# Attention units of all token groups in one pipeline: scores and values in one TensorE section

## The chip, the cores and the metric

The kernel runs on one core of one Trainium2 chip. The metric is the device time of one execution in microseconds. The kernel before takes 826.89 us, the median of three runs (826.69 to 827.46).

## What is computed

The reference is masked attention followed by a token mixer and a channel mixer, for 8 batches of 576 tokens, 8 heads of 64. Heads 0 to 3 see the last 32 positions ("local"), heads 4 to 7 every 32nd earlier position ("strided"):

```python
scores = (1.0 / np.sqrt(D)) * np.matmul(q, k.transpose(0, 1, 3, 2))
mask_local = (rel >= 0) & (rel < 32)
mask_strided = (rel >= 0) & (pos[None, :] % 32 == pos[:, None] % 32)
attn = softmax(where(mask, scores, -1e9))
x = (attn @ v).transpose(0, 2, 1, 3).reshape(B, S, H * D)
h = np.maximum(x.transpose(0, 2, 1) @ w_tok1, 0.0) @ w_tok2
u = x + h.transpose(0, 2, 1)
out = u + np.maximum(u @ w_ch1, 0.0) @ w_ch2
```

## The kernel before

The channel mixer is most of the work. The 4608 tokens are cut into 9 groups of 512. For each group, mlp() (line 668) runs 12 up-projections (up_proj, L680) and 12 down-projections (down_proj, L699), of 12 matmuls of 128x512 each, since every fp32 product is made of three products of split halves. An up-projection accumulates in one of two PSUM banks of the pool ps_h; its result is read by ScalarE (gh, L685) and then by VectorE (gl, L686), and used by the down-projection two steps later. Four further banks hold the down-projection's sums, and the last two are the pool ps_t.

Between these matmuls mlp() has 48 slots for each group, four for each step fc: slot 4fc in the middle of up_proj(fc+2), 4fc+1 behind it and ahead of the reads gh and gl, 4fc+2 in the middle of down_proj(fc), and 4fc+3 behind it. Everything else for the next batch is inserted there by at(slot, function), and each engine runs its instructions in just this order, since the schedule is manual: attention units, the token mixer (tok1 at slots 31 to 41, tok2 around it), the loads of x, and in group 0 the conversion of the weights (convert at even slots, fetch at odd ones; ScalarE and VectorE rebuild and split each 128x512 piece, and a DMA on SyncE's queue brings the next).

An attention unit is a Python generator (local_unit L194, strided_unit L254) over two or three blocks of 128 rows and two heads. Its steps are: load q and k; scores, 24 or 48 small matmuls (L81) into two ps_t banks; on VectorE the masked scores with their minimum (L167) and on ScalarE the exponentials (L170), for each block and head; reciprocal of the sums and load of v; transposes on TensorE (L84) with a copy on ScalarE (L191); values, again 24 or 48 small matmuls (L81) into two ps_t banks; a product with the reciprocals on VectorE (L237, L291) into the tile ax; a store to DRAM. A later load_x reads the stored rows as x of the next batch. The framework puts two engines' accesses to one PSUM bank one behind the other.

In groups 0 and 1 there are eight units each, four strided and four local, one every three slots from slot 4. Unit k's scores stand at slot 4+3k, together with the transposes of unit k-1, which go into the free columns of the same two banks; its values stand five slots after its scores, in a section of their own. Groups 2 to 6 have three, three, three, three and two local units, one every five slots from slot 0, with the values eight slots after the scores. A stretch of TensorE work of this kind between matmuls of the mixer is called a section below. Batches 3 to 7 have their strided heads on GpSimd and VectorE (L345, L346, L393, L395), which don't use TensorE. The loads of x are issued from SyncE's queue at slots 28 and 31 (24 and 27 from group 2), behind the stores that they need. The output tiles of a group (result, L716) are taken from GpSimd's product tiles and from the local units' tile lv.

Of the kernel before, what the change touches and what calls it, by code (L numbers as in the profile page):

```python
# [26 lines left out]
P = 128  # L27
# [58 lines left out]

class Bank:
# [6 lines left out]
def attn_mixer_kernel(ctx, tc, qT, kT, vw, qs, ks, vs, qsT, ksT, vsP, mask, words, outT):  # L94
# [62 lines left out]
    def new_scores(work):  # L157
        small = [work.tile([P, 16], F32, name=name)[:, :2 * UC].rearrange("p (c j) -> p c j", j=2) for name in ("am", "az")]
        return work.tile([P, UC, 2, 64], F32, name="as"), *small
# [34 lines left out]
    def local_unit(pool, work, p, hp, c0, n, into=None, got=None):  # L194
# [28 lines left out]
        for t in range(4 * n):  # L223
            c, a = divmod(t, 4)
            for j in range(2):
                av[j].by.matmul(
                    av[j].of[32 * a:32 * a + 32, 64 * c:64 * c + 64],
                    pT[64 * j:64 * j + 64, 32 * t:32 * t + 32], v_t[64 * j:64 * j + 64, t], start=True, stop=True)
        x_t = new_out(work)
# [24 lines left out]
    def strided_unit(pool, work, b, hp, half, got=None):  # L254
# [28 lines left out]
        for t in range(UT):  # L283
            c, a = divmod(t, 2)
            for j in range(2):
                av[j].by.matmul(
                    av[j].of[64 * a:64 * a + 64, 64 * c:64 * c + 64],
                    pT[64 * j:64 * j + 64, P * c + 64 * a:P * c + 64 * a + 64], v_t[64 * j:64 * j + 64, t], start=True, stop=True)
        x_t = new_out(work)
# [246 lines left out]
    with tc.tile_pool(name="first", bufs=2) as first, \  # L536
# [68 lines left out]
        for k in range(n + 3):  # L605
            if k >= 3:
                units[k - 3].send(banks[k - 3])
            if 0 <= k - 2 < n:
# [52 lines left out]
    ps_h = Banks(tc, ctx.enter_context(tc.tile_pool(name="ps_h", bufs=2, space=PSUM, reuse_waits="tile")))  # L661
# [6 lines left out]
    def mlp(grp, us, inserts):  # L668
# [3 lines left out]
        def up_proj(fc, mid=lambda: None):  # L672
            fs = slice(P * fc, P * fc + P)
            ph = ps_h.tile("h")
# [31 lines left out]
        def out_tile(cc):  # L706
            if cc < NCC - 1:
                o_t = product(pools["sp"], (SPROD, D))
            else:
                o_t = late.tile([P, 4 * UC, D], F32, name="lv")[:, :GT // D]  # L710
            return o_t.rearrange("p a b -> p (a b)")
# [54 lines left out]
    def do_load(b, part):  # L766
        if part == 0:
            state["x"] = xp.tile([P, NSC, DM], F32, name="x", bufs=1)
            if b < NPE:
                load_x(state["x"], b, 1)  # L770
            load_x(state["x"], b, 0, 0, 2)
        else:
            load_x(state["x"], b, 0, 2)
            if b >= NPE:
                load_x(state["x"], b, 1)
# [39 lines left out]
    def group_units(b):  # L815
# [6 lines left out]
        return st[:1] + [u for k in range(4) for us_ in (st[1:], loc) for u in us_[k:k + 1]]  # L822

    made = {}
    all_units = [group_units(g + 1) for g in range(B - 1)] + [[], []]
    all_live = [[None] * len(u) for u in all_units]

    def load(g, k):
        all_live[g][k] = all_units[g][k]()
        next(all_live[g][k])  # L830

    for g in range(NG):
# [6 lines left out]
        def pair():  # L839
            return [ps_t.bank() for _ in range(2)]  # L840

        b = g + 1
        if b < B:
            units, live = all_units[g], all_live[g]
            first_, tick, half_tick, ahead = (4, 3, 2, 3) if g < 2 else (0, 5, 3, 4)
            def qk(k, live=live):
                banks = pair()
                u = live[k] if k < len(live) else None
                if u:
                    u.send(banks)  # L850
# [171 lines left out]
```

## Time and profile before

| | us |
|---|---|
| median of three runs | 826.89 |
| the profiled execution | 826.54 |
| its span, first to last instruction | 824.8 |
| TensorE busy | 799.4 (97%) |
| VectorE busy | 477.4 (58%) |
| ScalarE busy | 260.8 (32%) |
| GpSimd busy | 252.3 (31%) |
| chain that ended last, TensorE's share | 87% |

Matmuls overlap in the record: one of 128x512 is shown at 0.39 us, but the next starts some 0.227 us after it. What a section costs is therefore read from starts: from the last matmul of the mixer ahead of it to the first or second one behind it, less what these matmuls would take in a row.

### The profile page before, as it was taken

To read this page: it belongs to the slowest core of one execution; us is meant where nothing else is said; L and a number is where in the kernel's file an instruction comes from. 1 tells how busy PE (TensorE), PEld (TensorE's weight loads), DVE (VectorE), ACT (ScalarE), POOL (GpSimd) and SP (SyncE) were. 2 spreads that over 40 slices of the span, in tenths; PEclk is the share of its full clock that TensorE was granted. 3 is DMA by queue.
4 is the path that set the end of the run, shared out by engine and by line. 5 is a ranking of instruction groups with operands and counts; after the bars stand their busy time and mean duration, and the time that the engine had idled before them with its cause. 6 is when DMAs were issued, how large, how long until landed. Compare 5 with 4: busy or idle time off the path is not lost.

```text
span 824.8 us, 16436 instructions
## 1 busy us (share of the span) xinstructions
PE 799.4 (97%) x6360; PEld 649.3 (79%) x6360; DVE 477.4 (58%) x1694; ACT 260.8 (32%) x803; POOL 252.3 (31%) x258
## 2 busy tenths in 40 slices
PE   6899889999999999999999999999999999999998
PEld 5666668877788788878887888788878888888886
DVE  4887775445467668766786676766775324113122
ACT  6777773244322312231224121322131221101110
POOL 2300000042201792279426762578238100000000
PEclk9999999999999999999999999999999999999999
DMA  9546762234524231232314140515021301001001
GB/s 362 183 141 209 227 215 61 85 128 143 141 68 147 80 94 58 87 126 55 112 53 147 40 142 25 173 39 141 1 91 40 92 1 52 1 0 39 14 1 51
DMA packets 61905, 79.65 MB, mean 97 GB/s; under 512 B 16676, under 2 KB 47268, under 8 KB 61828
## 3 DMA queue, kind: packets, MB, share of 16 engines
q1 hardware_dynamic: 60404, 74.14, 28.6%
q0 software_dynamic: 1136, 4.06, 1.3%
q8 instruction: 50, 0.82, 0.4%
q10 hardware_dynamic: 288, 0.40, 0.1%
q14 instruction: 27, 0.22, 0.1%
HBM read 59.97 MB, written 18.48 MB: 95 GB/s over the span
## 4 chain that ended last, share of the span: by engine, by line
PE 87%; ACT 5%; DMA 3%; DVE 3%; issue 1%; SPq 0%; ACTq 0%; DVEq 0%
PE acc L699 34%; PE h L680 33%; PE t L81 19%; ACT as L170 2%; PE t L84 2%; DMA lv<-in_vw 1%; ACT w_raw L124 1%; DMA x<-ax 1%; DMA mask_sb<-in_mask 1%; DMA ek<-in_ksT 1%; ACT gh L685 1%; ACT w_a L122 0%; DMA w_raw<-in_words 0%; DVE w1l L153 0%; DVE gl L686 0%
## 5 line engine op out<-in xcount | busy, mean ns | idle before, releaser
L393 POOL TENSOR_TENSOR sprod<-sv,ss 128x512 f32<-128x512 f32 (+9 forms) x150 | 136.3, 949 | 137.0 <-DVE ss L369 101.1
L680 PE MATMUL h<-uh,w1h 128*128 128x512 f32 x432 | 171.9, 398 | 1.4 <-DVE ul L488 1.4
L699 PE MATMUL acc<-gh,w2h 128*128 128x512 f32 x432 | 172.5, 399 | 0.0
L699 PE MATMUL acc<-gh,w2l 128*128 128x512 f32 x432 | 168.7, 391 | 0.0
L680 PE MATMUL h<-uh,w1l 128*128 128x512 f32 x432 | 168.6, 390 | 0.0
L699 PE MATMUL acc<-gl,w2h 128*128 128x512 f32 x432 | 168.6, 390 | 0.0
L680 PE MATMUL h<-ul,w1h 128*128 128x512 f32 x432 | 168.5, 390 | 0.0
L686 DVE SCALAR_TENSOR_TENSOR gl<-h,gh 128x512 fp32r<-128x512 f32 x108 | 74.2, 687 | 132.4 <-ACT gh L685 131.8
L685 ACT ACTIVATE gh<-h 128x512 fp32r<-128x512 f32 x108 | 64.8, 600 | 257.4 <-PE h L680 257.3
L345 POOL TENSOR_TENSOR sprod<-sk,sq 128x512 f32<-128x512 f32 x80 | 101.9, 1305 | 135.6 <-DVE ss L346 96.3
L680 PEld LDWEIGHTS h<-uh,w1h 128*128 128x128 f32 x432 | 81.1, 188 | 19.5 <-DVE ul L488 2.2
L699 PEld LDWEIGHTS acc<-gh,w2l 128*128 128x128 f32 x432 | 81.1, 188 | 17.4
L680 PEld LDWEIGHTS h<-uh,w1l 128*128 128x128 f32 x432 | 81.1, 188 | 17.2
L699 PEld LDWEIGHTS acc<-gh,w2h 128*128 128x128 f32 x432 | 81.2, 188 | 16.6
L680 PEld LDWEIGHTS h<-ul,w1h 128*128 128x128 f32 x432 | 81.2, 188 | 15.8
L699 PEld LDWEIGHTS acc<-gl,w2h 128*128 128x128 f32 x432 | 81.3, 188 | 15.3
L395 DVE TENSOR_REDUCE so<-sprod 128x64 f32<-128x512 f32 (+9 forms) x150 | 73.5, 524 | 12.6 <-POOL sprod L393 11.8
L170 ACT ACTIVATE as<-as,am 128x64 f32<-128x64 f32 x216 | 72.3, 337 | 25.2 <-DVE am L167 23.0
L488 DVE TENSOR_TENSOR ul<-t,uh 128x512 fp32r<-128x512 f32 (+7 forms) x64 | 29.1, 457 | 71.7 <-ACT uh L487 71.7
L487 ACT CAST uh<-t 128x512 fp32r<-128x512 f32 (+7 forms) x64 | 25.6, 404 | 116.7 <-PE t L81 116.7
L346 DVE TENSOR_REDUCE ss<-sprod 128x8 f32<-128x512 f32 x80 | 52.2, 670 | 12.4 <-POOL sprod L345 12.2
L167 DVE CUSTOM_DVE_ANT_0 as<-t,mask_sb 128x64 f32<-128x64 f32 x216 | 34.5, 221 | 35.2 <-ACT as L191 21.9
(103 smaller groups left out, 928.7 us busy)
## 6 DMA issues: line engine op xcount, KB each, us to landing
w_raw<-in_words SPq DMA_DIRECT2D x21, 512.0 KB, 4.5
out_t<-sprod SPq DMA_DIRECT2D x27, 256.0 KB, 2.2
lv<-in_vw SPq DMA_DIRECT2D x18, 384.0 KB, 4.3
lk<-in_kT SPq DMA_DIRECT2D x18, 208.0 KB, 3.4
x<-xl SPq DMA_DIRECT2D x14, 256.0 KB, 4.4
lq<-in_qT SPq DMA_DIRECT2D x18, 192.0 KB, 3.1
xl<-ax SPq DMA_DIRECT2D x18, 192.0 KB
sq<-in_qs SPq DMA_DIRECT2D x5, 576.0 KB
```

The lines of the kernel that those rows point to most:

```text
L81: self.tc.stamp_issue_order_token(self.tc.nc.tensor.matmul(*args, **how).ins, self.pool.name)
L167: nc.vector.tensor_tensor_reduce(out=s_t[:, c, j, :], in0=sc[j].of[:, 64 * c:64 * c + 64], in1=mask_sb[:, m, :], scale=-SCALE, scalar=TOP, ...
L170: nc.scalar.activation(out=s_t[:, c, j, :], in_=s_t[:, c, j, :], func=AF.Exp, bias=m_t[:, c, j:j + 1], scale=-1.0, accum_out=z_t[:, c, j:j ...
L345: nc.gpsimd.tensor_tensor(out=pr, in0=k_t[:, n0:n0 + n], in1=q_t[:, i:i + 1].to_broadcast([P, n, D]), op=ALU.mult)
L346: return [lambda: nc.vector.tensor_reduce(out=s_t[:, i, n0:n0 + n], in_=pr, axis=AX.X, op=ALU.add)]
L393: nc.gpsimd.tensor_tensor(out=pr, in0=v_t[:, d0:d1, :n], in1=s_t[:, n - 1:n, :n].to_broadcast([P, d1 - d0, n]), op=ALU.mult)
L395: todo.append(lambda n=n, d0=d0, d1=d1, pr=pr: nc.vector.tensor_reduce(out=o_t[:, n - 1, d0:d1], in_=pr, axis=AX.X, op=ALU.add))
L488: nc.vector.tensor_tensor(out=ul, in0=pu, in1=uh.bitcast(F32), op=ALU.subtract)
L680: nc.tensor.matmul(ph, l[:, cc, fs], r, start=(cc == 0 and k == 0), stop=(cc == NCC - 1 and k == 2))
L685: nc.scalar.activation(out=gh, in_=ph, func=AF.Relu)
L686: nc.vector.scalar_tensor_tensor(out=gl, in0=ph, scalar=0.0, in1=gh.bitcast(F32), op0=ALU.max, op1=ALU.subtract)
L699: nc.tensor.matmul(acc[cc], l[:, fc, cs], r, start=(fc == 0 and k == 0), stop=(fc == NFC - 1 and k == 2))
```

## The change

All 30 units of all groups become one list with one list of 32 sections: slots 4, 7, ..., 31 of group 0, 4, 7, ..., 25 of group 1, then 4, 11 and 18 of groups 2 to 5, and 4 and 11 of group 6. Strided and local units of groups 0 and 1 now alternate strictly. Section n has, in TensorE's order, the values of unit n-2 in columns 0 to 191 of two ps_t banks, the scores of unit n in columns 192 to 383 of the same banks and, up to section 16, the transposes of unit n-1 in the bank of ps_h that the up-projections don't use at that moment. Behind that, VectorE takes the scores first and the values' product second. From unit 16 on the scores of unit k and the values of unit k-1 share a section, and the transposes stand alone in a ps_t bank, four slots after the scores (seven after those at slot 18).

The two banks of ps_h get names, h0 and h1. Turns.next() alternates between them; Turns.spare(turn) hands out the bank that is not in use: at slots 4fc and 4fc+1 (turn 0) the one whose up-projection has been read before, at 4fc+2 and 4fc+3 (turn 1) the same, with the turn flipped, so that the next up-projection goes into the bank of the up-projection just before it.

Loads of q and k move from three (or four) slots ahead of the scores to four (five); v is loaded two (three) slots after the scores, as before. The loads of x stand at slots 28, 30 and 33 in groups 0 and 1 (24, 27, 27 later), with the strided half second. A group's last values in group 0 stand at slot 31 and the strided ones at 28 (before: 30 and 24). The minima am have one buffer and the sums az three in these pools (before: two each). Output tiles are taken from the tiles xh and xlo of tok1.

```diff
--- before.py
+++ after.py
@@ -84,6 +84,19 @@
         self.tc.stamp_issue_order_token(self.tc.nc.tensor.transpose(*args).ins, self.pool.name)
 
 
+class Turns(Banks):
+
+    last = 0
+
+    def next(self):
+        self.last ^= 1
+        return self.tile(f"h{self.last}")
+
+    def spare(self, turn):
+        self.last ^= turn
+        return self.bank(f"h{self.last if turn else self.last ^ 1}")
+
+
 class Bank:
 
     def __init__(self, by, of):
@@ -155,7 +168,8 @@
 
 
     def new_scores(work):
-        small = [work.tile([P, 16], F32, name=name)[:, :2 * UC].rearrange("p (c j) -> p c j", j=2) for name in ("am", "az")]
+        bufs = {"am": 1, "az": 3} if work is pools.get("wk") else {"am": 4, "az": 4}
+        small = [work.tile([P, 16], F32, name=name, bufs=bufs[name])[:, :2 * UC].rearrange("p (c j) -> p c j", j=2) for name in ("am", "az")]
         return work.tile([P, UC, 2, 64], F32, name="as"), *small
 
     def new_out(work):
@@ -226,6 +240,7 @@
                 av[j].by.matmul(
                     av[j].of[32 * a:32 * a + 32, 64 * c:64 * c + 64],
                     pT[64 * j:64 * j + 64, 32 * t:32 * t + 32], v_t[64 * j:64 * j + 64, t], start=True, stop=True)
+        yield
         x_t = new_out(work)
         cs = slice(P * hp, P * hp + P)
 
@@ -286,6 +301,7 @@
                 av[j].by.matmul(
                     av[j].of[64 * a:64 * a + 64, 64 * c:64 * c + 64],
                     pT[64 * j:64 * j + 64, P * c + 64 * a:P * c + 64 * a + 64], v_t[64 * j:64 * j + 64, t], start=True, stop=True)
+        yield
         x_t = new_out(work)
         for j in range(2):
             nc.vector.tensor_tensor(
@@ -605,6 +621,7 @@
         for k in range(n + 3):
             if k >= 3:
                 units[k - 3].send(banks[k - 3])
+                next(units[k - 3])
             if 0 <= k - 2 < n:
                 b0, b1 = banks[k - 2]
                 next(units[k - 2])
@@ -658,7 +675,7 @@
 
     up = ctx.enter_context(tc.tile_pool(name="up", bufs=3, reuse_waits="tile"))
     ps_acc = ctx.enter_context(tc.tile_pool(name="ps_acc", bufs=1, space=PSUM, reuse_waits="tile"))
-    ps_h = Banks(tc, ctx.enter_context(tc.tile_pool(name="ps_h", bufs=2, space=PSUM, reuse_waits="tile")))
+    ps_h = Turns(tc, ctx.enter_context(tc.tile_pool(name="ps_h", bufs=1, space=PSUM, reuse_waits="tile")))
     ps_t = Banks(tc, ctx.enter_context(tc.tile_pool(name="ps_t", bufs=2, space=PSUM, reuse_waits="tile")))
 
     convert()
@@ -671,7 +688,7 @@
 
         def up_proj(fc, mid=lambda: None):
             fs = slice(P * fc, P * fc + P)
-            ph = ps_h.tile("h")
+            ph = ps_h.next()
             for cc in range(NCC):
                 if cc == NCC // 2:
                     mid()
@@ -704,11 +721,7 @@
                 f()
 
         def out_tile(cc):
-            if cc < NCC - 1:
-                o_t = product(pools["sp"], (SPROD, D))
-            else:
-                o_t = late.tile([P, 4 * UC, D], F32, name="lv")[:, :GT // D]
-            return o_t.rearrange("p a b -> p (a b)")
+            return xp.tile([P, GT], F32, name=("xh", "xlo")[cc % 2])
 
         def store(cc, o_t):
             nc.sync.dma_start(out=outT[P * cc:P * cc + P, GT * grp:GT * grp + GT], in_=o_t)
@@ -766,13 +779,11 @@
     def do_load(b, part):
         if part == 0:
             state["x"] = xp.tile([P, NSC, DM], F32, name="x", bufs=1)
-            if b < NPE:
-                load_x(state["x"], b, 1)
             load_x(state["x"], b, 0, 0, 2)
+        elif part == (1 if b < NPE else 2):
+            load_x(state["x"], b, 1)
         else:
             load_x(state["x"], b, 0, 2)
-            if b >= NPE:
-                load_x(state["x"], b, 1)
 
     def do_tok1(b):
         if "tok1" not in state:
@@ -819,15 +830,54 @@
         for p, hp, c0, n in local_order[:4 if b < 3 else 3]:
             loc.append(lambda p=p, hp=hp, c0=c0, n=n: local_unit(pools["late"], pools["wk"], p, hp, c0, n))
         del local_order[:len(loc)]
-        return st[:1] + [u for k in range(4) for us_ in (st[1:], loc) for u in us_[k:k + 1]]
+        return [u for k in range(4) for us_ in (st, loc) for u in us_[k:k + 1]]
 
     made = {}
-    all_units = [group_units(g + 1) for g in range(B - 1)] + [[], []]
-    all_live = [[None] * len(u) for u in all_units]
-
-    def load(g, k):
-        all_live[g][k] = all_units[g][k]()
-        next(all_live[g][k])
+    units = [u for g in range(B - 1) for u in group_units(g + 1)]
+    live = [None] * len(units)
+    nu = 16
+    sections = [4 + 3 * k for k in range(10)] + [NS + 4 + 3 * k for k in range(8)]
+    sections += [NS * g + i for g in range(2, 6) for i in (4, 11, 18)] + [NS * 6 + i for i in (4, 11)]
+    places = {}
+
+    def put(t, f):
+        places.setdefault(t, []).append(f)
+
+    def load(k):
+        live[k] = units[k]()
+        next(live[k])
+
+    def section(new, out, mid, turn):
+        banks = [ps_t.bank() for _ in range(2)]
+        if out is not None:
+            live[out].send(banks)
+        if new is not None:
+            live[new].send([Bank(ps_t, bank.of[:, 64 * UC:]) for bank in banks])
+        if mid is not None:
+            transposes(mid, ps_h.spare(turn))
+        if new is not None:
+            next(live[new])
+        if out is not None:
+            next(live[out])
+
+    def transposes(k, bank):
+        live[k].send([(bank, 0, UC)])
+
+    for k in range(len(units)):
+        close = k < nu
+        t, t1 = (sections[k + (not close) + d] for d in (0, 1))
+        put(t - (4 if close else 5), lambda k=k: load(k))
+        put(t + (2 if close else 3), lambda k=k: next(live[k]))
+        if not close:
+            put(t + (7 if t % NS == 18 else 4), lambda k=k: transposes(k, ps_t.bank()))
+    for n, t in enumerate(sections):
+        if n <= nu:
+            new, out, mid = n if n < nu else None, n - 2 if n > 1 else None, n - 1 if n else None
+        elif n == nu + 1:
+            new, out, mid = nu, nu - 1, None
+        else:
+            new, out, mid = n - 1 if n - 1 < len(units) else None, n - 2, None
+        put(t, lambda new=new, out=out, mid=mid, turn=t % 4 > 1: section(new, out, mid, turn))
 
     for g in range(NG):
 
@@ -836,56 +886,26 @@
         def at(i, f):
             ins.setdefault(i, []).append(f)
 
-        def pair():
-            return [ps_t.bank() for _ in range(2)]
-
+        for i in range(NS):
+            for f in places.pop(NS * g + i, ()):
+                at(i, f)
         b = g + 1
         if b < B:
-            units, live = all_units[g], all_live[g]
-            first_, tick, half_tick, ahead = (4, 3, 2, 3) if g < 2 else (0, 5, 3, 4)
-            def qk(k, live=live):
-                banks = pair()
-                u = live[k] if k < len(live) else None
-                if u:
-                    u.send(banks)
-                if k:
-                    live[k - 1].send([(banks[0], 256, 2), (banks[1], 256, 1)])
-                if u:
-                    next(u)
-
-            def z(k, live=live):
-                next(live[k])
-
-            def av(k, live=live):
-                live[k].send(pair())
-
-            for k, u in enumerate(units):
-                t = first_ + tick * k
-                if t >= ahead:
-                    at(t - ahead, lambda k=k, g=g: load(g, k))
-                at(t, lambda k=k: qk(k))
-                at(t + half_tick, lambda k=k: z(k))
-                at(t + tick + half_tick, lambda k=k: av(k))
-            at(first_ + tick * len(units), lambda: qk(len(live)))
             if g == 0:
                 for i in range(-2, 37, 2):
                     at(i, convert)
                     at(i + 1, fetch)
                 at(NS - 1, staging_ends)
-            last = first_ + tick * len(units) + half_tick
-            i0, i1 = (31, 36) if g < 2 else (27, 32)
-            assert i0 > last
-            for part in range(2):
-                at(i0 - 3 * (1 - part), lambda part=part: do_load(b, part))
+            i1 = 36 if g < 2 else 32
+            for part, i in enumerate((28, 30, 33) if g < 2 else (24, 27, 27)):
+                at(i, lambda part=part: do_load(b, part))
             for c in range(NSC + 1):
                 at(i1 + c if c else i1 - 1, lambda: do_tok1(b))
             at(i1 + NSC, tok1_ends)
             for i in range(2):
                 at(((43, 46) if g < 2 else (39, 43))[i], lambda i=i: do_tok2(b, False, (2 * i, 2 * i + 1)))
             if g == 1:
-                at(last + 1, third_ends)
-            if g and all_units[g + 1]:
-                at(44, lambda g=g: load(g + 1, 0))
+                at(26, third_ends)
         for i, t in enumerate((1, 3) if g < 2 else (20, 22) if b < B else (4, 7) if g < B else ()):
             at(t, lambda i=i: do_tok2(g, True, (2 * i, 2 * i + 1)))
         turns = []
@@ -894,8 +914,8 @@
             turns += [(2 + min(k, ROUNDS), "av") for k in range(ROUNDS + 2)]
         if g and g + 2 < B:
             at(0 if g == 1 else 3, lambda: state.update({("qk", g + 2): strided_loads(pools["sp"], g + 2)}))
-            places = [*range(3, 33, 2), 39] if g == 1 else [*range(21, 31), 38, 39, 41, 42, 43, 46]
-            turns += [(i, "qk") for i in [*places, 47]] + [(i, "few") for i in range(i1 + 1, i1 + 6)] + [(33, "v")]
+            at_qk = [*range(3, 33, 2), 39] if g == 1 else [*range(21, 31), 38, 39, 41, 42, 43, 46]
+            turns += [(i, "qk") for i in [*at_qk, 47]] + [(i, "few") for i in range(i1 + 1, i1 + 6)] + [(33, "v")]
 
         def turn(i, what, g=g):
             if what == "qk":
```

## Rows read from the trace of the kernel before

**Rows 1.** Page, part 1 and the slices of part 2: TensorE's busy time.

```profile
PE 799.4 (97%) x6360; PEld 649.3 (79%) x6360; DVE 477.4 (58%) x1694; ACT 260.8 (32%) x803; POOL 252.3 (31%) x258
...
PE   6899889999999999999999999999999999999998
```

**Rows 2.** Timeline of TensorE: first and last of 36 matmuls in a row.

```profile
154.14 0.39 PE L680 MATMUL h<-uh,w1h 128*128 128x512 f32 x1
...
162.07 0.40 PE L680 MATMUL h<-uh,w1l 128*128 128x512 f32 x1
```

**Rows 3.** Timeline of TensorE: a section of values alone, group 3.

```profile
358.22 0.39 PE L680 MATMUL h<-uh,w1l 128*128 128x512 f32 x1
358.54 0.72 PE L81 MATMUL t<-lv,as 64*32 64x64 f32 x48
359.20 0.50 PE L680 MATMUL h<-uh,w1h 128*128 128x512 f32 x1
359.53 0.39 PE L680 MATMUL h<-ul,w1h 128*128 128x512 f32 x1
```

**Rows 4.** Timeline of TensorE: a section of scores with transposes, group 3.

```profile
352.98 0.39 PE L680 MATMUL h<-uh,w1l 128*128 128x512 f32 x1
353.30 0.72 PE L81 MATMUL t<-lk,lq 64*32 64x64 f32 x48
353.96 0.55 PE L84 MATMUL t<-ident,as 128*128 128x128 f32 x3
...
354.57 0.39 PE L699 MATMUL acc<-gl,w2h 128*128 128x512 f32 x1
```

**Rows 5.** Timeline of TensorE: a section of transposes alone, group 3.

```profile
370.66 0.39 PE L699 MATMUL acc<-gh,w2l 128*128 128x512 f32 x1
370.90 0.49 PE L84 MATMUL t<-ident,as 128*128 128x128 f32 x3
...
371.46 0.39 PE L680 MATMUL h<-ul,w1h 128*128 128x512 f32 x1
```

**Rows 6.** Timeline of TensorE: group 0, around slot 4, then around slot 31.

```profile
65.85 0.40 PE L680 MATMUL h<-uh,w1l 128*128 128x512 f32 x1
...
124.36 0.39 PE L680 MATMUL h<-uh,w1h 128*128 128x512 f32 x1
```

**Rows 7.** Waits of TensorE in that stretch: waited for, total us, times, longest.

```profile
PE t L81 <- DMA ek<-in_ksT: 1.6, 2, 0.9
PE t L81 <- ACT w2h L151: 1.1, 1, 1.1
...
PE t L81 <- DVE ax L291: 1.0, 2, 0.6
...
PE t L81 <- ACT as L170: 0.2, 1, 0.2
```

**Rows 8.** Busy time of each engine in that stretch, clock, DMA share, GB/s.

```profile
65.85:124.53 58.68, 52.18 (x633) 38.45 (x632) 44.21 (x171) 44.65 (x133) 0.00 (x0) 1.00 0.67 212
```

**Rows 9.** ScalarE's groups in that stretch: busy, mean ns, idle before them.

```profile
L170 ACT ACTIVATE as<-as,am 128x64 f32<-128x64 f32 x40 | 13.4, 336 | 6.4 <-DVE am L167 6.3
```

**Rows 10.** Timelines of three engines: an up-projection read, the next one started.

```profile
89.13 0.57 ACT L685 ACTIVATE gh<-h 128x512 fp32r<-128x512 f32 x1
...
89.73 0.69 DVE L686 SCALAR_TENSOR_TENSOR gl<-h,gh 128x512 fp32r<-128x512 f32 x1 [1.92 <-ACT gh L685]
...
90.67 0.50 PE L680 MATMUL h<-uh,w1h 128*128 128x512 f32 x1
```

**Rows 11.** Waits of TensorE in group 1's sections (169 to 224 us).

```profile
PE t L81 <- DMA lv<-in_vw: 1.4, 2, 0.9
```

**Rows 12.** Waits of VectorE, whole span.

```profile
DVE as L167 <- ACT as L191: 21.9, 18, 2.1
```

**Rows 13.** Waits of SyncE's queue, 60 to 131 us.

```profile
SPq L415 <- DMA xl<-ax: 4.6, 1, 4.6
```

**Rows 14.** DMA issues, 65 to 125 us: count, KB each, us to landing.

```profile
x<-xl SPq DMA_DIRECT2D x1, 256.0 KB, 5.4
```

## The prediction

> **What bounds the kernel now.** I read the page's busy times and slices first. TensorE is busy for 97% of the span, and its slices stand at nine tenths or more except at the two ends and in slices 5 and 6, inside group 0 [rows 1]. A change that takes TensorE work or TensorE waits away therefore comes straight off the time; one that helps another engine does not. Next I read the timeline of TensorE for the pace of the mixer: 36 matmuls in a row start from 154.14 to 162.07, so one costs 7.93 / 35 = 0.2267 us [rows 2]. With this pace the price of every section can be read from starts, and the same pace leaves over what group 0 loses to waits. The waits by engine, the busy times of that stretch and the queue's waits come last, since they tell what could stand in the way.
>
> **Sections: what joining them saves.** A section of values alone runs from the matmul at 358.22 to the second one behind it at 359.53: 1.31 - 2 x 0.2267 = 0.86 us. Its 48 small matmuls fill 358.54 to 359.20, 0.66 us. The remaining 0.20 are edges: 0.32 instead of 0.23 going in, 0.33 instead of 0.23 behind it [rows 3]. Scores with transposes cost 1.59 - 0.45 = 1.14, again with 0.66 us for the 48 small matmuls, so the transposes add 0.28 [rows 4]. Transposes alone cost 0.80 - 0.45 = 0.35 [rows 5].
>
> Before, there are 30 score sections (23 of them with transposes), 30 value sections and 7 with transposes alone. Afterwards there are 32 sections, 16 with transposes, and 14 with transposes alone. That is 60 - 32 = 28 pairs of edges fewer: 28 x 0.20 = 5.6 us. The transposes go from 23 x 0.28 + 7 x 0.35 = 8.9 to 16 x 0.28 + 14 x 0.35 = 9.4, 0.5 more. Together -5.1 us, all of it on TensorE.
>
> No row has values followed directly by scores, so the price of that join needs bounds. The nearest rows are the joins of scores and transposes: joined 1.14, apart 0.86 + 0.35 = 1.21, so that join saved only 0.07 [rows 3 to 5]. That is the lower end: 28 x 0.07 - 0.5 = 1.5 us. The upper end takes the 0.06 us that the transposes lose behind another tile shape (0.30 against 0.24 from their start to the next matmul's) as lost at each exit too: 28 x 0.26 - 0.5 = 6.8. I take 0.20, because values and scores of one section have one shape here: the units alternate, so n-2 and n are of one kind, and 48 matmuls of one shape run on without a gap inside a section.
>
> The Trainium skill, TensorEngine Tiling (Array Packing), section Key Properties, says that changing the tiling mode, and not merely the tile, drains the engine. That fits the rows: the edges are paid where the shape changes. By it the join of values and scores is free of them and the sum is as taken; by the join of scores and transposes alone it would be the lower end.
>
> **Group 0: waits.** From slot 4 to slot 31, from the matmul at 65.85 to that at 124.36, lie 58.51 us [rows 6]. They hold 163 matmuls of the mixer (the one at 65.85, half a projection of 6 and 13 whole ones of 12), 163 x 0.2267 = 36.95; 21.6 us are sections and waits. The view of waits names eight kinds, 6.5 us in all, each at the head of a section: loads of q, k and v that came late, and ps_t banks still held by VectorE's product of the section one slot before (releasers ax) [rows 7]. The change works against both. Sections stand three slots apart instead of one and two in turn, q and k are asked for a slot earlier, and v has four slots instead of three. So all 6.5 could go.
>
> What is late next is ScalarE: 44.65 us busy in these 58.68, VectorE 44.21 [rows 8]. Both keep their work, and the stretch gets the scores of a ninth unit: six exponentials at 0.336, 2.0 us [rows 9], so 46.7 for ScalarE. Without waits TensorE would need 58.5 - 6.5 - 1.4 (seven joins) = 50.6 us. ScalarE would then have to be busy for 92% of it, in order, behind scores that it waits for already (6.3 us) [rows 9]. I take 5.0 of the 6.5 us as gained and keep 0 and 6.5 as ends.
>
> The transposes in an idle bank of ps_h add a wait of their own. At turn-1 slots (7, 10, 19, 22, 31) the next up-projection uses the bank of the one just before. In the worst case shown, the reads of one are late: gh at 89.13, gl at 89.73 and busy to 90.42, and the next up-projection starts at 90.67 [rows 10]. It would have waited 0.0 us by this row, with 0.25 to spare. Queued behind such a wait is the whole of TensorE. I cost it at nothing, within the 1.5 us kept; the cover is the down-projection between the two, 12 x 0.2267 = 2.7 us. At turn-0 slots 13 and 25 the same 2.7 us cover ScalarE's copy.
>
> **Group 1.** The two waits for lv, 1.4 us, come from a unit of the same kind right before it, whose v held the only buffer [rows 11]. With strict alternation the buffer is free three slots earlier: -1.4 us, with 0 as the other end.
>
> **The bank conflict.** VectorE's scores wait for ScalarE's copy of the transposes in the same bank, 21.9 us in 18 waits [rows 12]. Up to section 16 that wait goes. TensorE's own waits don't name it, so I count no gain; it is part of why I let ScalarE go up to 92%.
>
> **What is moved on the queues.** In group 0 the last strided values go from slot 24 to 28 and the load of their x from 28 to 30; the last local values go from 30 to 31, behind them the scores of a further unit, and the load from 31 to 33. SyncE's queue waits 4.6 us for that store to land before the load is issued [rows 13], and 5.4 pass until it has landed [rows 14]. Values, VectorE's scores and product ahead of the store (about 2.7 us from section's start, an estimate from 0.66 us twice and six reads) make 2.7 + 0.4 + 4.6 + 0.4 + 5.4 = 13.5 us; from slot 31 to the third chunk's matmuls at slot 39 TensorE has 8 x 6 x 0.2267 = 10.9, the section's 1.6 and two chunks of tok1 at 1.4 (estimated from 6 matmuls), 15.3 in all, less 1.3 for the split of the chunk. That leaves 0.5 us, and the four loads of the strided half stand ahead in the same queue. I take 0.7 us as lost, ends 0 and 3. The out tiles leave GpSimd's products and lv; nothing on TensorE waits for them, so nothing is counted. From group 2 on TensorE waits for nothing in sections, and their slots move to places where the mixer covers the reads; +0, up to 1 for the section at 18, which tok2 follows two slots later on the same banks.
>
> **Sum.** -5.1 - 5.0 - 1.4 + 0.7 = -10.8. On the profiled execution's 826.54: 815.7. The median stands 0.35 above it, so 816.0 (rounded).
>
> **Rivals.** First, ScalarE takes the place of the waits: group 0 gives nothing back and the loads of x cost 1.5. For it: 92%. Against it: ScalarE has 58.7 - 44.7 = 14 us idle there today, 6.3 of them for VectorE's scores, which come earlier without the shared bank. -5.1 - 1.4 + 1.5 = -5.0: 821.9. The Trainium skill's tiling page, section PSUM Bottleneck, points the same way: faster TensorE work doesn't speed up the reading of PSUM.
>
> Second, all waits go and their restarts with them: -5.1 - 6.5 - 1.4 - 2.5 (the edges of waits below those listed, an estimate) = -15.5: 811.4.
>
> Third, the join costs what scores and transposes cost: -1.5 - 5.0 - 1.4 + 0.7 = -7.2: 819.7.
>
> Fourth, slower: the idle bank isn't idle. If ScalarE runs late, each of the five turn-1 sections of group 0 holds TensorE until gl is done. At 2.5 us each that is 12.5 us, with no gain from group 0's waits: -5.1 - 1.4 + 12.5 = +6.0: 832.9. It decides from 6.5 / 5 = 1.3 us each. For it: the margin of 0.25 us [rows 10]. Against it: a late TensorE lets ScalarE catch up, so the delay doesn't add up.
>
> Fifth, the change doesn't do what it says, waits for loads and banks simply move: within 0.2% of 826.9.
>
> **How the numbers follow.** A measurement of this kernel can tell about 0.2%, 1.7 us, from no change. Forecast 0.50, ScalarE 0.17, all waits gone 0.14, dear join 0.08, slower 0.07, nothing 0.04. Faster: 0.50 + 0.17 + 0.14 + 0.08 = 0.89; same 0.04; slower 0.07. The range 810.8 to 822.0 takes in the first four and leaves out the slower case, no change and a little beyond, some 0.15.
>
> **What would show it.** Joined sections with 0.2 us less than their parts; no row of TensorE waiting on lv or ax; the stretch from slot 4 to slot 31 at 52 us; ScalarE above 85% in it. Wrong: waits of TensorE at up-projections with gl (L686) as the releaser, at tok1 with x or xh, or sections whose values and scores cost 1.5 us and more with edges between them.

## The result and the profile after

The kernel after takes 816.39 us, the median of four runs (815.2 to 817.87), against 827.17 for the kernel before beside it (826.69 to 828.08): a ratio of 0.9871, 95% interval 0.985 to 0.9893, so 10.8 us less. The profiled execution of after took 817.87 us, the longest of its four; its span is 816.1, 8.7 less than the span before. Line numbers below are those of after: up-projection L697, its reads gh L702 and gl L703, down-projection L716, exponentials L184, copy of the transposes L205, subtract xlo L446, GpSimd's products L361.

The page of after, busy times, TensorE's slices and its granted clock in these slices (before: [rows 1], with the clock at 9 in all 40 slices):

```profile
PE 791.5 (97%) x6360; PEld 648.3 (79%) x6360; DVE 479.0 (59%) x1694; ACT 258.0 (32%) x777; POOL 252.2 (31%) x258
...
PE   6899999999999999999999999999999999999998
...
PEclk9899999999999999999999999999999999999999
```

The number of matmuls is the same and TensorE is busy for 7.9 us less. Slices 5 and 6, below nine tenths before, reach them now. TensorE bounds the kernel as it did. In slice 2, ahead of slot 4, the granted clock is lower than before; the part on the prediction comes back to it.

**A joined section**, timeline of TensorE, group 2:

```profile
258.31 0.39 PE L697 MATMUL h<-uh,w1l 128*128 128x512 f32 x1
258.63 0.72 PE L81 MATMUL t<-lv,as 64*32 64x64 f32 x48
259.16 0.71 PE L81 MATMUL t<-lk,lq 64*32 64x64 f32 x48
259.80 0.50 PE L697 MATMUL h<-uh,w1h 128*128 128x512 f32 x1
260.14 0.39 PE L697 MATMUL h<-ul,w1h 128*128 128x512 f32 x1
```

Values and scores together cost 260.14 - 258.31 - 2 x 0.2267 = 1.38 us. Apart they cost 0.86 each (values: [rows 3]; scores alone: 0.86 too, in group 2 of before), 1.72. A join saves 0.34, more than the 0.20 of the forecast and more than its upper bound of 0.26. The row shows why: the 48 values last 0.53 us from their start to the start of the scores, but 0.66 where a matmul of another shape follows [rows 3]. The 0.66 that the prediction took for work holds 0.13 of waiting for the change of shape.

**Group 0, slot 4 to slot 31**: busy time by engine, and TensorE's waits in that window (answers to [rows 6 to 8]).

```profile
67.00:120.34 53.34, 49.42 (x624) 37.58 (x622) 41.68 (x176) 43.24 (x138) 0.00 (x0) 1.00 0.74 238
```

```profile
PE h L697 <- DVE gl L703: 3.3, 4, 2.0
PE h L697 <- ACT as L205: 0.5, 1, 0.5
```

The stretch fell from 58.51 to 53.34 us. The eight kinds of waits of before are gone, the loads of k and the product ax among them. In their place TensorE waits at up-projections for gl: four times here and a fifth time, 1.61 us, right behind the window, at slot 31. They are the five turn-1 slots, whose transposes stand in the idle bank of ps_h: 0.91, 0.18, 1.99, 0.20 and 1.61, 4.9 in all. The long ones are at slots 7, 19 and 31, where the next up-projection follows at once; at slots 10 and 22 six matmuls (1.4 us) stand between. The timeline shows how the longest came about:

```profile
95.87 1.35 ACT L137 COPY w_raw<-w_raw 128x512 uint8<-128x512 uint8 x1
...
96.95 0.70 ACT L702 ACTIVATE gh<-h 128x512 fp32r<-128x512 f32 x1
...
97.68 0.69 DVE L703 SCALAR_TENSOR_TENSOR gl<-h,gh 128x512 fp32r<-128x512 f32 x1 [1.43 <-ACT gh L702]
...
98.43 0.50 PE L697 MATMUL h<-uh,w1h 128*128 128x512 f32 x1 [1.99 <-DVE gl L703]
```

The read gh stands in ScalarE's queue behind a byte copy of a weight piece (1.35 us), gl waits for gh, and the next up-projection now waits for gl, because it goes into the same bank. A byte copy of 1.35 to 1.38 us stands right ahead of gh at all five places (from 71.66, 78.85, 95.87, 103.05 and 120.99).

**Group 1** gives 5.4 us. The two waits for lv [rows 11] are gone, 1.4. Seven joins are 2.4. Some 0.7 is one section of scores that now stands in group 0, at slot 31. Most of the rest are two sections of values for lv that cost 1.10 and 1.06 in before, without a listed wait, instead of 0.85.

**tok1 of groups 2 to 5** is the part that no step of the prediction names. Its first section cost 1.36 in every group before; after, it costs 1.79, 1.98, 2.05 and 2.15, 2.5 us more in all. TensorE waits there for the subtract xlo (waits of TensorE, whole span):

```profile
PE t L81 <- DVE xlo L446: 1.4, 4, 0.5
```

The subtract's durations (min, median, max in ns), before and then after:

```profile
L430 DVE TENSOR_TENSOR xlo<-x,xh x35: 672/692/1778, 129.1 to 667.4; 128x512 fp32r<-128x512 f32 x35
```

```profile
L446 DVE TENSOR_TENSOR xlo<-x,xh x35: 674/691/3609, 130.5 to 658.7; 128x512 fp32r<-128x512 f32 x35
```

In the timelines of VectorE and GpSimd of after, the first subtract of group 2 is issued at 303.87 while a product runs, and ends at 307.42; GpSimd's eleven products run on without a gap to 306.87:

```profile
303.87 3.55 DVE L446 TENSOR_TENSOR xlo<-x,xh 128x512 fp32r<-128x512 f32 x1
```

```profile
292.98 13.89 POOL L361 TENSOR_TENSOR sprod<-sk,sq 128x512 f32<-128x512 f32 x11 [0.26 <-DVE so L411]
```

### The profile page after: what moved, and what is told of

Its sections match the earlier page's. It is cut to its first block, busy times and chain, and to the rows that moved or that the text cites. A ratio compares the mean times of both kernels' runs of the same rounds, so it can differ in the third digit from the quotient of the medians.

```text
span 816.1 us, 16384 instructions
## 1 busy us (share of the span) xinstructions
PE 791.5 (97%) x6360; PEld 648.3 (79%) x6360; DVE 479.0 (59%) x1694; ACT 258.0 (32%) x777; POOL 252.2 (31%) x258
## 4 chain that ended last, share of the span: by engine, by line
PE 81%; ACT 5%; DMA 5%; DVE 5%; issue 1%; SPq 1%; POOL 0%; ACTq 0%; DVEq 0%; POOLq 0%
PE acc L716 31%; PE h L697 31%; PE t L81 18%; ACT as L184 2%; DMA x<-xs 2%; DVE xlo L446 2%; DMA w_raw<-in_words 2%; ACT w_raw L137 1%; PE t L84 1%; DMA mask_sb<-in_mask 1%; SPq L431 1%; DMA xs<-so 1%; ACT w_a L135 1%; DVE gl L703 1%; ACT xh L445 0%
## 5 line engine op out<-in xcount | busy, mean ns | idle before, releaser
L697 PE MATMUL h<-uh,w1h 128*128 128x512 f32 x432 | 171.9, 398 | 6.8 <-DVE gl L703 4.9
L716 PE MATMUL acc<-gh,w2h 128*128 128x512 f32 x432 | 170.5, 395 | 0.0
L716 PE MATMUL acc<-gh,w2l 128*128 128x512 f32 x432 | 168.5, 390 | 0.0
L697 PE MATMUL h<-uh,w1l 128*128 128x512 f32 x432 | 168.5, 390 | 0.0
L716 PE MATMUL acc<-gl,w2h 128*128 128x512 f32 x432 | 168.4, 390 | 0.0
L697 PE MATMUL h<-ul,w1h 128*128 128x512 f32 x432 | 168.4, 390 | 0.0
L703 DVE SCALAR_TENSOR_TENSOR gl<-h,gh 128x512 fp32r<-128x512 f32 x108 | 74.3, 688 | 138.8 <-ACT gh L702 138.8
L361 POOL TENSOR_TENSOR sprod<-sk,sq 128x512 f32<-128x512 f32 x80 | 101.5, 1306 | 137.2 <-DVE ss L362 94.3
L702 ACT ACTIVATE gh<-h 128x512 fp32r<-128x512 f32 x108 | 64.9, 601 | 224.8 <-PE h L697 224.8
L697 PEld LDWEIGHTS h<-uh,w1h 128*128 128x128 f32 x432 | 81.1, 188 | 26.2 <-DVE gl L703 6.5
L697 PEld LDWEIGHTS h<-uh,w1l 128*128 128x128 f32 x432 | 81.1, 188 | 17.3
L716 PEld LDWEIGHTS acc<-gh,w2l 128*128 128x128 f32 x432 | 81.1, 188 | 17.3
L716 PEld LDWEIGHTS acc<-gh,w2h 128*128 128x128 f32 x432 | 81.2, 188 | 16.3
L716 PEld LDWEIGHTS acc<-gl,w2h 128*128 128x128 f32 x432 | 81.2, 188 | 15.8
L697 PEld LDWEIGHTS h<-ul,w1h 128*128 128x128 f32 x432 | 81.2, 188 | 15.7
L184 ACT ACTIVATE as<-as,am 128x64 f32<-128x64 f32 x216 | 72.3, 338 | 66.1 <-DVE am L181 66.1
```

The lines of the kernel that those rows point to most:

```text
L184: nc.scalar.activation(out=s_t[:, c, j, :], in_=s_t[:, c, j, :], func=AF.Exp, bias=m_t[:, c, j:j + 1], scale=-1.0, accum_out=z_t[:, c, j:j ...
L361: nc.gpsimd.tensor_tensor(out=pr, in0=k_t[:, n0:n0 + n], in1=q_t[:, i:i + 1].to_broadcast([P, n, D]), op=ALU.mult)
L697: nc.tensor.matmul(ph, l[:, cc, fs], r, start=(cc == 0 and k == 0), stop=(cc == NCC - 1 and k == 2))
L702: nc.scalar.activation(out=gh, in_=ph, func=AF.Relu)
L703: nc.vector.scalar_tensor_tensor(out=gl, in0=ph, scalar=0.0, in1=gh.bitcast(F32), op0=ALU.max, op1=ALU.subtract)
L716: nc.tensor.matmul(acc[cc], l[:, fc, cs], r, start=(fc == 0 and k == 0), stop=(fc == NFC - 1 and k == 2))
```

## The experiments

The theory: three things set the result, the join of shapes (sections), the reads behind ScalarE's weight work in group 0, and GpSimd's products in front of tok1. The rivals are in the expectations. All runs are compared with the kernel before beside them, so ratios are set against after's 0.9871; the medians of the kernel before beside them lie between 825.6 and 827.6.

**Transposes between values and scores** (groups 0 and 1): the same work with two more changes of shape.

```diff
         if out is not None:
             live[out].send(banks)
-        if new is not None:
-            live[new].send([Bank(ps_t, bank.of[:, 64 * UC:]) for bank in banks])
         if mid is not None:
             transposes(mid, ps_h.spare(turn))
+        if new is not None:
+            live[new].send([Bank(ps_t, bank.of[:, 64 * UC:]) for bank in banks])
```

> The changed kernel, but in each section of groups 0 and 1 the transposes stand between the values and the scores (order values, transposes, scores). No instruction more or less. Theory A (a run of small matmuls of one shape pays its edges once, and every change of shape pays them again): the 14 sections with all three parts lose the join of 0.34 us and get back only some 0.07 for the transposes' other neighbour, so 3 to 4.5 us slower than 816.4, that is 819.5 to 821, and in group 1 a section of 48 + 3 + 48 small matmuls costs 1.9 to 2.0 us instead of 1.66. Theory B (the gain is fewer stops of the mixer's stream, whatever stands inside a section): unchanged within 1 us, and the section at 1.66 to 1.73.

Measured: 818.9 us (816.97 to 821.17), ratio 0.9899 (0.9877 to 0.992). Timeline of TensorE, a local section of group 1, first in this kernel, then in after:

```profile
175.83 0.39 PE L716 MATMUL acc<-gh,w2l 128*128 128x512 f32 x1
176.15 0.72 PE L81 MATMUL t<-lv,as 64*32 64x64 f32 x48
176.81 0.55 PE L84 MATMUL h<-ident,as 128*128 128x128 f32 x3
177.28 0.72 PE L81 MATMUL t<-lk,lq 64*32 64x64 f32 x48
177.94 0.50 PE L697 MATMUL h<-uh,w1h 128*128 128x512 f32 x1
178.28 0.39 PE L697 MATMUL h<-ul,w1h 128*128 128x512 f32 x1
```

```profile
185.45 0.39 PE L697 MATMUL h<-uh,w1l 128*128 128x512 f32 x1
185.77 0.72 PE L81 MATMUL t<-lv,as 64*32 64x64 f32 x48
186.30 0.71 PE L81 MATMUL t<-lk,lq 64*32 64x64 f32 x48
186.94 0.55 PE L84 MATMUL h<-ident,as 128*128 128x128 f32 x3
187.24 0.47 PE L716 MATMUL acc<-gh,w2h 128*128 128x512 f32 x1
187.56 0.39 PE L716 MATMUL acc<-gl,w2h 128*128 128x512 f32 x1
```

From first to last row, less 0.45, that is 2.00 against 1.66 us; a strided section of group 1 costs 1.71 against 1.35. So 0.34 to 0.36 for the same 99 or 51 matmuls, and where transposes follow the values, these fill 0.66 again. The section's price is theory A's. The total rose by 2.5 in the medians, less than expected: the waits for gl fell from 4.9 to 2.1, as TensorE comes later, and a new wait of 1.9 for a weight piece (w_raw, L146) took part of that back.

**Values apart again** (groups 2 to 6): the last values of a group's pipeline are sent alone two slots ahead. The edit undoes 13 joins, not the 12 of the expectation.

```diff
+        if n > nu + 1:
+            put(t - 2, lambda out=out: section(None, out, None, 0))
+            out = None
         put(t, lambda new=new, out=out, mid=mid, turn=t % 4 > 1: section(new, out, mid, turn))
```

> The changed kernel, but in groups 2 to 6 the values stand alone, two slots ahead of the scores that they shared a section with; groups 0 and 1 are as changed. TensorE waits for nothing in these sections, so this prices the join by itself: 12 sections of values and scores (1.37 us) become two of 0.86 us each. Theory A (the join saves 0.34 us): 12 x 0.34 = 4.1 us, 820.5. The price as predicted (0.20 us of edges): 12 x 0.20 = 2.4, 818.8. No saving by the join at all: 816.4.

Measured: 821.89 us (820.74 to 823.14), ratio 0.9941 (0.9922 to 0.996), 5.5 us above after. Timeline of TensorE, values alone:

```profile
365.25 0.40 PE L697 MATMUL h<-uh,w1l 128*128 128x512 f32 x1
365.58 0.72 PE L81 MATMUL t<-lv,as 64*32 64x64 f32 x48
366.23 0.50 PE L697 MATMUL h<-uh,w1h 128*128 128x512 f32 x1
366.56 0.39 PE L697 MATMUL h<-ul,w1h 128*128 128x512 f32 x1
```

That is 0.86 us again. Values and scores apart cost 0.34 to 0.35 more than joined, 13 x 0.345 = 4.5 us. The other 1.0 is in the trace too: from the end of group 1 to the last matmul this kernel takes 5.5 us more than after (564.5 against 558.9). Priced up to the next section instead of the second matmul behind, a section of values or scores alone costs 0.91 to 0.92 here and a joined one 1.40 in after, since the matmuls behind a section start somewhat further apart; why is not shown. In before, values alone cost mostly 0.88 by that measure. The join is confirmed by a second edit in other groups, at 0.34 or more.

**Transposes of turn-1 slots later**, alone at slot 4fc+4, in the other bank of ps_h: no up-projection can wait for gl on their account.

```diff
-        put(t, lambda new=new, out=out, mid=mid, turn=t % 4 > 1: section(new, out, mid, turn))
+        late_t = t % 4 > 1 and mid is not None
+        put(t, lambda new=new, out=out, mid=None if late_t else mid: section(new, out, mid, 0))
+        if late_t:
+            put(t // 4 * 4 + 4, lambda mid=mid: transposes(mid, ps_h.spare(0)))
```

> The changed kernel, but at the nine slots 4fc+2 and 4fc+3 of groups 0 and 1 the transposes are taken out of the section and stand alone in the middle of the next up-projection (slot 4fc+4), in the other bank of ps_h, so that no up-projection goes into the bank of the one just before it. Theory A (the five waits of up-projections for gl, 4.9 us, come from the flipped turn alone): they are gone, the nine separate sections of transposes cost 9 x 0.07 = 0.6 us and waits for gl at the transposes are at most 1 us, so 812 to 813.5. Rival (TensorE in group 0 is held by ScalarE's and VectorE's work as a whole, and the wait only shows up at the bank): the waits move to the transposes or the next section, and the time stays within 1 us of 816.4.

Measured: 816.39 us (815.96 to 817.23), ratio 0.9875 (0.9856 to 0.9895), the same as after. TensorE's waits, whole span:

```profile
PE t L81 <- ACT as L205: 5.9, 6, 1.7
```

No row names gl any more. Values now wait for ScalarE's copy of their transposes instead (1.2 us in 2 waits in after). ScalarE's timeline ahead of the longest of these waits (1.70 us, until the values start at 83.89):

```profile
82.07 0.34 ACT L184 ACTIVATE as<-as,am 128x64 f32<-128x64 f32 x1
...
82.40 0.61 ACT L164 CAST w2h<-w_a 128x512 fp32r<-128x512 f32 x1
82.91 0.67 ACT L135 ACTIVATE w_a<-w_raw 128x512 f32<-128x512 f32 x1
83.48 0.35 ACT L205 COPY as<-h 128x256 f32<-128x256 f32 x1
```

The wait moved to another place in ScalarE's queue: here the section's exponentials and two steps of a weight piece stand ahead of the copy, not a byte copy. So theory A, that the time comes back once the bank's turn is gone, falls. That the byte copies made gh late is not shown by this run, but by the next.

**Byte copies on GpSimd**: the copy L137 of every second weight piece leaves ScalarE.

```diff
-        yield from joined(raw, whole[:, :n], "dve" if k % 2 else "act")
+        yield from joined(raw, whole[:, :n], "dve" if k % 2 else "pool")
```

> The changed kernel, but the byte copy of every second weight piece in group 0 (128x512 bytes, 1.37 us) is GpSimd's instead of ScalarE's. Theory A (the up-projections wait for gl because ScalarE reads them late, behind a piece's byte copy: gh starts 1 to 2 us after its projection is done at slots 7, 19 and 31): the waits for gl fall from 4.9 us to under 1.5, the stretch from slot 4 to slot 31 from 53.3 to about 50.5 us, 812.5 to 814. Rival (VectorE and the chain of a piece's steps are the limit, which gain nothing, since GpSimd's copy takes as long, 1.33 us): waits stay at 4 us and more, with VectorE's step behind the copy as releaser; within 1 us of 816.4.

Measured: 814.78 us (813.96 to 815.55), ratio 0.9866 (0.9852 to 0.988). In group 0 it does what the theory says: the waits for gl fall from 4.9 to 0.7, and slot 4 to slot 31 lasts 49.5 us (67.17 to 116.69), 3.8 less than in after. TensorE's waits, whole span:

```profile
PE t L81 <- DVE hl L662: 0.9, 1, 0.9
PE t L81 <- ACT w_a L135: 0.7, 1, 0.7
...
PE h L697 <- DVE gl L703: 0.7, 1, 0.7
PE t L81 <- DMA lk<-in_kT: 0.4, 1, 0.4
```

But not all of the 3.8 us stays. At slot 31 the waits for w_a and lk take 1.1 us in place of gl's 1.6. Between 33 and 66 us, ahead of the stretch, where weight pieces are converted too, TensorE waits 3.4 us for ul and hl instead of 2.2, and behind the last matmul another 0.4 is added. That leaves 3.8 + 0.5 - 1.2 - 0.4 = 2.7 by the traces. The spans of the two profiled executions differ by more (812.2 against 816.1), but the one of after had a lower granted clock early on (see below). In the total the medians say 1.6 us, the ratios 0.4, and 814.78 is above the expected 812.5 to 814: how much of the gain is left is not settled by this run.

**Two products fewer ahead of tok1** (groups 2 to 5): GpSimd's products of slots 29 and 30 move to 44 and 45.

```diff
-            at_qk = [*range(3, 33, 2), 39] if g == 1 else [*range(21, 31), 38, 39, 41, 42, 43, 46]
+            at_qk = [*range(3, 33, 2), 39] if g == 1 else [*range(21, 29), 38, 39, 41, 42, 43, 44, 45, 46]
```

> The changed kernel, but in groups 2 to 5 the two GpSimd products issued at slots 29 and 30 stand at slots 44 and 45. Theory A (TensorE's waits for xlo at tok1 in these groups, about 0.43 + 0.62 + 0.69 + 0.79 = 2.5 us, come from the subtract xlo, which takes up to 3.6 us instead of 0.69 while GpSimd's products run without a gap): xlo is back at about 0.7 us, the first section of tok1 costs 1.36 us in each of the four groups, 813.5 to 814.5. Rival (x arrives too late, since TensorE gets to tok1 earlier and the loads don't): the first section stays at 1.8 to 2.1 us and the time at 816.4.

Measured: 813.61 us (812.5 to 814.28), ratio 0.9839 (0.9817 to 0.9862), 2.8 below after. The subtract's durations:

```profile
L446 DVE TENSOR_TENSOR xlo<-x,xh x35: 679/693/1143, 129.2 to 655.2; 128x512 fp32r<-128x512 f32 x35
```

tok1's first sections cost 1.36, 1.35, 1.36 and 1.36 again. The 2.5 us are GpSimd's products, as theory A has it.

**Two product buffers instead of three**: what ends the time in which GpSimd keeps VectorE out?

```diff
-        return pool.tile([P, SPROD * D], F32, name="sprod", bufs=3)
+        return pool.tile([P, SPROD * D], F32, name="sprod", bufs=2)
```

> Compared with the kernel after, GpSimd's products (tile sprod) have two buffers instead of three. In the kernel after, the subtract xlo is issued at 303.87 us behind a product of GpSimd and ends only after three further products have ended without a gap (the last at 306.86); GpSimd then has no free product buffer left, because VectorE's reduces stand behind the subtract. Theory A: GpSimd keeps VectorE's subtract out for as long as it has a free buffer, so with two buffers it stops one product (1.3 us) earlier: the longest subtract falls from 3.6 to at most 2.4 us, tok1's first sections in groups 2 to 5 come back from 1.8 to 2.15 us to 1.36 to 1.5, and the time falls by 1.5 to 2.5 us, to about 814. Theory B: how long the subtract is kept out hangs on the moment at which it is issued and not on buffers: some subtracts still take over 3 us and the time stays at 816.4 within 1. Either way fewer buffers may delay the products by up to some tenths of a microsecond each, which TensorE does not wait for.

Measured: 816.41 us (814.51 to 817.37), ratio 0.9864 (0.984 to 0.9888), the same as after. The subtract's durations, and VectorE and GpSimd around the first of them (timelines):

```profile
L446 DVE TENSOR_TENSOR xlo<-x,xh x35: 675/691/2455, 127.7 to 657.5; 128x512 fp32r<-128x512 f32 x35
```

```profile
301.90 0.62 DVE L362 TENSOR_REDUCE ss<-sprod 128x7 f32<-128x448 f32 x1 [0.43 <-POOL sprod L361]
...
303.78 3.05 DVE L446 TENSOR_TENSOR xlo<-x,xh 128x512 fp32r<-128x512 f32 x2
```

```profile
291.82 13.86 POOL L361 TENSOR_TENSOR sprod<-sk,sq 128x512 f32<-128x512 f32 x11 [0.68 <-DVE so L411]
```

The longest subtract is shorter by 1.15 us, about one product, so on the length theory A holds: GpSimd keeps the subtract out until it has no free buffer left. In each of groups 2 to 5 three products are finished and unread when the long subtract of after ends, and two when that of this kernel ends. On the time it fails: the sections cost 1.75 and 1.90 in groups 2 and 3, hardly less than the 1.79 and 1.98 of after. TensorE reached this tok1 1.16 us earlier than in after (305.78 against 306.94), but the subtract was issued at 303.78 against 303.87, because VectorE's reduces ahead of it each wait for a product. Up to here GpSimd sets the pace, 1.26 us a product (13.86 / 11); the subtract ends 0.55 us behind the last product in both kernels, and it was fewer products that helped.

**Byte copies on GpSimd and two products fewer**, the two edits above in one kernel:

```diff
+        yield from joined(raw, whole[:, :n], "dve" if k % 2 else "pool")
...
+            at_qk = [*range(3, 33, 2), 39] if g == 1 else [*range(21, 29), 38, 39, 41, 42, 43, 44, 45, 46]
```

> The byte copy on GpSimd and the two products of groups 2 to 5 moved to slots 44 and 45, together. The two waits lie in different groups, so the gains should add: 813.6 less what the byte copy alone gives (2.5 to 4 us by theory A), 809.5 to 811. If the byte copy gives nothing, 813.6.

Measured: 811.97 us (811.35 to 812.25), ratio 0.9831 (0.9818 to 0.9845), a little above the expected 809.5 to 811. Of the 4.4 us below after, 2.8 are the products. For the byte copy 1.6 are left in the medians, as in its own run, not the 2.5 to 4 expected; the ratios, 0.9831 and 0.9839, do not separate the two kernels.

**The same with the transposes later**, all three edits:

```diff
+        yield from joined(raw, whole[:, :n], "dve" if k % 2 else "pool")
...
+            put(t // 4 * 4 + 4, lambda mid=mid: transposes(mid, ps_h.spare(0)))
...
+            at_qk = [*range(3, 33, 2), 39] if g == 1 else [*range(21, 29), 38, 39, 41, 42, 43, 44, 45, 46]
```

> As the kernel before this one in the list, but with the transposes of the nine sections at 4fc+2 and 4fc+3 alone in the middle of the next up-projection. Theory A (ScalarE's lateness is what is paid, at whichever place the copies or the reads are needed; with the byte copy gone there is little of it): no gain over leaving the transposes in the section, 0 to 1 us slower, since nine sections more cost 9 x 0.07 us. Rival (the flipped turn is a cost of its own): 1 us and more faster.

Measured: 811.89 us (809.66 to 812.77), ratio 0.9828 (0.981 to 0.9845), the same as the one above: with gl's waits down to 1.1 us there is nothing left to move. Values wait 2.9 us for copies here. These two are the fastest kernels of the case, 1.7% below before and half a per cent below after.

## Why the prediction was right, and where only in the sum

The forecast was 816.0, the measurement 816.39. Its steps came out as follows, in terms of the two profiled executions.

- **Joins: right in kind, mis-sized.** -(28 x 0.345 - 0.5) = -9.2 us instead of -5.1. The step that failed is the one that split a section into "work" of 0.66 and edges of 0.20; the drain of 0.13 behind the last small matmul lay inside the 0.66. The transposes were sized rightly: 1.66 - 1.38 = 0.28 behind a joined section. The nearest row taken for the lower bound, the join of scores and transposes, has a change of shape in it and was no guide. The Trainium skill, TensorEngine Tiling (Array Packing), Key Properties, says that a change of tiling mode drains TensorE; with 0.34 to 0.36 us for each pair of changes taken out or put in, two experiments agree with it.
- **Group 0's waits: wrong.** Predicted -5.0 of 6.5. The old ones all went, but 3.8 us of new ones stand in the stretch and 1.6 at slot 31: 6.5 - 5.4 = 1.1 us gained. The stretch's own 5.2 us are 2.7 of waits and 7 x 0.345 = 2.4 of joins; that it ended near the forecast of 52 was two errors against each other. The failed step is "I cost it at nothing": the row with 0.25 us to spare [rows 10] has no byte copy ahead of gh. The fourth rival named this wait and its five places; its size was 1.0 us each on average, below the 1.3 from which it would have decided, and its counterargument has support too: where TensorE came later, in the experiment with transposes between values and scores, these waits fell to 2.1. ScalarE was busy for 43.24 of 53.34 us, 81%, not above 85%; its ninth unit cost what was worked out (46 exponentials, 15.4 us, against 13.4 [rows 9]). It was not the share that made it late but the order of its queue. So the sign of being wrong that the prediction named, up-projections that wait for gl, did appear. The experiment with later transposes shows the first rival's mechanism, ScalarE in the place of the old waits, beside the fourth's.
- **Group 1's waits: right**, -1.4.
- **Loads of x in group 0: +0.7 predicted, 0 found.** tok1's first section costs 1.36 in both. The wait of SyncE's queue for the store was 0.9 us instead of the 4.6 on which the estimate stood [rows 13].
- **Not seen: +2.5** in tok1 of groups 2 to 5. The prediction let the scores and values of these groups move "to places where the mixer covers the reads; +0", and looked only at sections. What fell out of cover was the subtract.

The sum of what was found: -9.2 - 1.1 - 1.4 + 0 + 2.5 = -9.2. From slot 4 on, the two profiled executions differ by 9.8 (758.9 and 749.1 us); most of the 0.6 between are the two dear sections of group 1. Ahead of slot 4 both kernels give TensorE the same work, and yet slot 4 starts 1.15 us later in after. There the granted clock stood at 0.5 (1.2 GHz) from 25.11 to 31.93 us in after, but only from 23.75 to 27.16 in before; in that stretch after falls from 0.5 us ahead to 1.1 behind. Shortly before, TensorE had stood 2.4 us waiting for ScalarE's exponentials (1.8 in before). So the 8.7 us between the profiled spans hold a difference in clock that this record doesn't tie to the change: in nine profiles with this pipeline slot 4's scores start between 65.90 and 67.70 (before: 66.31). The medians' 10.8 can't be split in this way; the interval of the ratio is 8.9 to 12.4 us and has room for both sums.

Against the prediction, the joins gave 4.1 more, the waits of group 0 gave 3.9 less, the loads of x cost 0.7 less and tok1 cost 2.5 more: errors of up to 4.1 us that nearly cancelled. The joins, the old waits and their places were foreseen; that the sum came within 0.4 us of the measurement is luck.

Open stays why GpSimd wins over VectorE in after and not before. Before, products ran at the same place, and the subtract took 0.83 and 1.78 us there while one product was stretched to 1.77: they took turns. After, the products stay at 1.30 to 1.36 and the subtract waits for two or three of them. The out tiles no longer share the products' buffers after the change; whether that or the instant of issue decides was not tried.

## What to carry to other kernels

Price a small section on TensorE by start to start with the same shape behind it: time that looks like work can be a drain, and joining sections of one shape saves it, while an order that changes shape in between gives it back. Before a buffer is reused earlier, look at what stands in its reader's queue in front of the read, at every place of reuse, not at one row with a margin. When TensorE gets faster, find the stages that another pair of engines paces (here GpSimd's products and VectorE's reduces) and move work out of the path of the one instruction there that TensorE needs.

## What the runs showed of the hardware

A two-input subtract of 128x512 on VectorE takes 0.69 us alone and up to 3.6 us in after (3.7 in two further runs) beside products of GpSimd that follow each other without a gap; it ended 0.55 us after the last product (306.87 and 307.42 in after, 305.68 and 306.23 with two buffers). The Trainium skill, SBUF — State Buffer, section "Who interferes with whom", says that such an instruction, with both inputs in SBUF, contends with a GpSimd one that reads SBUF, and that the shared port pair is an exclusive lock. The durations agree. That a waiting instruction of VectorE is passed by two products that start after it was issued (304.26 and 305.52, behind the one of 302.98) is more than that rule says, and is measured here.

A pair of changes between small tiles (64x32, 64x64) and full ones costs TensorE 0.34 to 0.36 us up to the second matmul behind, of which 0.13 lie behind the last small matmul and don't show in its own record (0.72 with and 0.72 without them).
